# Cross-attention and two expert layers on one core: the first 256 tokens' down projection and batch 0's scores in native float32

## The chip, the cores and the metric

The kernel runs on one core of a Trainium2 chip. Its time is the device time of one execution, in microseconds (us). PE multiplies matrices, DVE and ACT do the elementwise work, POOL issues the indirect transfers, and SP issues all other transfers from one queue in program order.

## The reference

For each of 8 batches and 8 heads, 512 tokens and 32 state rows of 64 numbers read each other by softmax attention; the two results are joined to 4352 rows of 512. A first layer and a routed second one follow:

```python
scores = scale * np.matmul(x, state.transpose(0, 1, 3, 2))
...
xread = np.matmul(a, state)
...
sread = np.matmul(a2, x)
...
h = x @ w_in                      # 512 -> 2048
r = np.maximum(h, 0.0)
g = r * r
return (g @ w_out)                # 2048 -> 512
...
expert_idx = np.argmax(logits, axis=1)        # 8 experts
    h = np.maximum(x[mask] @ w1[e], 0.0)      # 512 -> 1024
    out[mask] = gate_w[mask, None] * (h @ w2[e])
```

w_in and w_out arrive as float64. The result has to be good to float32, since a token's expert is an argmax.

## The kernel before

Most products are done in float16 in three terms: each float32 operand is scaled by a power of two and split into a high and a low half (`split`, lines 306 to 312: ACT writes the high half, DVE the low one), and PE sums high x high, high x low and low x high in one bank.

The front. `weights` loads w_in and w_out as 16 blocks of 1 MB of float64 (`block`). `to_f32` turns each into float32 by bit operations (DVE lines 750, 752 and 763, ACT line 747). For w_in, `wi_scale` takes a block's own scale (ACT square, a sum on PE at line 787, DVE) and `wi_block` splits it. For w_out, `wo_square` sums the squares of every block; only when all eight are known do `weights` and `tensor_scale` make the one scale, and `wo_split` makes the halves (ACT line 863, DVE line 304). The float32 form of w_out's block q lies where the halves of block q + 2 will stand.

`attention(b)` makes batch b's scores. The product of state and w_in is formed first (`state_w`, line 550, tile sw), so that the up projection of a unit of 256 tokens is attention weights (aT) x sw: 8 steps c of 12 matmuls of 256 columns (lines 1174 to 1176), each step in one of two banks u. `hidden` evicts a step (ACT line 1137), squares it (ACT lines 1141 and 1143 for units 0 and 1) and takes the low half (DVE line 1148) into g_h and g_l. `down1` multiplies a tile of 128 tokens by w_out in 48 matmuls of 512 columns (lines 1226 to 1228); two tiles make a unit, and there are 17 units. `route_tile` squares a result (line 1013), splits it and turns it for the gate; records go to DRAM. `experts` prepares the second layer's weights beside this: loads, squares (line 941), splits, and writes of the halves.

The second layer (`moe2`) gathers 128 records at a time, multiplies them by an expert's halves and scatters the rows; at the steps in `DRAINED`, seven of them, POOL then drains.

The order on each engine is not written down but planned: each part is a generator that tells the class `Plan` which engine it needs and for how long, and `Plan.run` always lets the step go that could start first, then the one of lower priority number. Transfers are planned to land 2 us and their bytes over 350 GB/s after they are issued. The plan decides only the order; on the chip every engine takes its queue in that order and waits where it must.

Of the kernel before, what the change touches and what calls it, by code (L numbers as in the profile page):

```python
# [10 lines left out]
F32 = mybir.dt.float32  # L11
# [23 lines left out]
DRAINED = range(6, FULL + HALF - LAST - 2, 4)  # L35
# [22 lines left out]
TINY = 0.18  # L58

# [173 lines left out]
def moe_kernel(  # L233
# [108 lines left out]
    tiny1 = const.tile([128, 1], F32, name="tiny1")  # L342
    nc.gpsimd.memset(tiny1, float(2.0 ** -112))
# [6 lines left out]
    cg = const.tile([128, B + 1], F32, name="cg")  # L350
    icg = const.tile([128, B + 1], F32, name="icg")
    swi = const.tile([128, NB], F32, name="swi")
    iswi = const.tile([128, NB], F32, name="iswi")
    smin = const.tile([128, 2], F32, name="smin")
    ismin = const.tile([128, 2], F32, name="ismin")
# [14 lines left out]
    g_h = mw.tile([128, KF, 512], F16, name="g_h")  # L370
    g_l = mw.tile([128, KF, 512], F16, name="g_l")
# [57 lines left out]
    def attention(b):  # L429
# [32 lines left out]
        plan.add(group_bound(b, p), 3 if b else 1.2)  # L462
# [134 lines left out]
    def state_side(b, xh, xl, sth, stl, scl):  # L597
# [9 lines left out]
        for C in range(2):  # L607
# [119 lines left out]
    def to_f32(q, dst, squares):  # L727

        raw = raws.pop(q)
        if not W64:  # L730
# [7 lines left out]
            V.tensor_copy(dst, w)  # L738
            yield ev("wosq", q - NB)
# [147 lines left out]
    def experts():  # L887
# [23 lines left out]
        def fetch():  # L911
            for n in range(4 * NE):
# [14 lines left out]
                ev("stage", n).set(when)  # L927
# [23 lines left out]
        for i in range(2 * NE):  # L951
# [5 lines left out]
            for q in range(4):  # L957
# [13 lines left out]
                phl_slots.release(t)  # L971
# [36 lines left out]
    def route_tile(i, ps, k_h, rc, st):  # L1008

        j = i % 4  # L1010
        rc = rc.bitcast(F16)
        yield act(600)
        nc.scalar.activation(out=rc[:, 0:512].bitcast(BF16), in_=ps, func=AF.Square, accum_out=st["f2"][:, j:j + 1])
# [4 lines left out]
        pow2(s2, st["is2"][:, j:j + 1], f2, 204)  # L1018
        yield from split(rc[:, 0:512], rc[:, 512:1024], ps, s2, 600)
# [108 lines left out]
    def hidden(u, c, ps, k_h):  # L1128
# [3 lines left out]
        yield ev("cg", g)  # L1132
        yield r_slots
# [57 lines left out]
    def down1():  # L1191
        for u in range(NU):
            g = u // 2
            for j in range(2):
                i = 2 * u + j
                if i == 0:
                    yield ev("prepared")
                if i % 4 == 0:
                    m, recs, k_r = 4 if g < B else 2, [], []
                    st = {"f2": small.tile([128, 4], F32, name="f2"),  # L1200
                          "is2": small.tile([128, 4], F32, name="is2"),
                          "lg": small.tile([128, 4, NE], F32, name="lg")}
                at = plan.now()
                yield rec_slots
                plan.cur[2] = max(at, plan.now())
                k_r.append(rec_slots.last())
                recs.append(mg.tile([128, REC], F32, name=f"rec{k_r[-1] % RECS}", bufs=1))
                yield "pool", 0.1
                nc.gpsimd.tensor_copy(recs[-1][:, 513:514].bitcast(I32), rid[:, i:i + 1])
                plan.cur[2] = at  # L1210
                ts = slice((i % 4) * 128, (i % 4) * 128 + 128)
                at = plan.now()
                yield d_slots
                plan.cur[2] = max(at, plan.now())
                ps, k_h = ps_d.tile([128, 512], F32, name="d"), d_slots.last()
                for q in range(4):
# [3 lines left out]
                    if u == 0:  # L1220
# [467 lines left out]
```

## Time and profile before

| | us |
|---|---|
| three runs: median (lowest, highest) | 1135.59 (1133.19, 1138.03) |
| profiled execution: its own time | 1135.78 |
| its span, first to last instruction | 1133.9 |
| PE busy | 1030.1 (91%) |
| DVE busy | 706.8 (62%) |
| ACT busy | 583.7 (51%) |
| POOL busy | 130.4 (12%) |

A busy PE need not be at its best, since its matmuls overlap; the spacing of their starts tells more than their lengths. A line such as 304 or 326 is a helper's, so tiles tell which step it serves. L12 is line 12 of the kernel before.

### The profile page before, as it was taken

The numbers are of one execution on the slowest core, as the hardware profiler recorded it, in microseconds if no ns is written. First come the engines' busy times: TensorE is split into PE (matmuls) and PEld (weight loads), VectorE is DVE, ScalarE is ACT, GpSimd is POOL, SyncE is SP. The second block draws the span as 40 slices with busy tenths as digits, with TensorE's granted clock in tenths as the row PEclk, the third lists the DMA queues.
The fourth block names the chain that finished last, engine by engine and source line by source line (L and its number), as shares of the span: only waits on it lengthen the run. The fifth ranks groups of instructions, "written<-read, shape, count | busy, mean of one in ns | idle before, by whom it ended". The sixth has DMA issues, their size and how long they took to land. (4 is left out here: it accounts for less than half of the span.)

```text
span 1133.9 us, 26458 instructions
## 1 busy us (share of the span) xinstructions
PE 1030.1 (91%) x10707; PEld 664.6 (59%) x10707; DVE 706.8 (62%) x1838; ACT 583.7 (51%) x959; POOL 130.4 (12%) x149
## 2 busy tenths in 40 slices
PE   2255799999999999899999999999999999999998
PEld 1134355555556556465565566677777777677775
DVE  6989786978878878688787686546322222222222
ACT  6579777776777877677777776311101111010110
POOL 0200000110100100001002010122112112112111
PEclk9579699999999999999999999999999999999999
DMA  9335457477584696574755477773696776784692
GB/s 353 122 153 130 153 103 233 96 196 190 135 264 104 197 265 150 157 191 133 229 133 178 159 227 247 236 201 95 187 312 172 215 212 188 187 267 129 187 281 103
DMA packets 160544, 211.76 MB, mean 187 GB/s; under 512 B 112225, under 2 KB 113505, under 8 KB 155170
## 3 DMA queue, kind: packets, MB, share of 16 engines
q1 hardware_dynamic: 152098, 182.94, 57.2%
q0 software_dynamic: 8320, 27.08, 7.2%
q8 instruction: 86, 1.41, 0.5%
q14 instruction: 40, 0.33, 0.1%
HBM read 257.92 MB, written 51.68 MB: 273 GB/s over the span
## 5 line engine op out<-in xcount | busy, mean ns | idle before, releaser
L1496 ACT ACTIVATE r<-u 128x512 f32<-128x512 f32 x70 | 41.8, 597 | 326.1 <-PE u L1542 302.0
L1226 PE MATMUL d<-wo_t,g_h 128*128 128x512 f16 x544 | 208.0, 382 | 1.7 <-ACT wo_t L863 0.8
L1227 PE MATMUL d<-wo_t,g_h 128*128 128x512 f16 x544 | 208.1, 383 | 1.2 <-DVE wo_t L304 1.2
L1228 PE MATMUL d<-wo_t,g_l 128*128 128x512 f16 x544 | 208.2, 383 | 0.0
L1174 PE MATMUL u<-aT,sw 128*128 128x256 f16 x512 | 141.6, 277 | 26.3 <-ACT r L1137 23.4
L1176 PE MATMUL u<-aT,sw 128*128 128x256 f16 x512 | 141.6, 276 | 0.5 <-DVE sw L304 0.5
L1175 PE MATMUL u<-aT,sw 128*128 128x256 f16 x512 | 141.6, 277 | 0.0
L1137 ACT ACTIVATE r<-u,cg 128x512 f32<-128x512 f32 x136 | 92.6, 681 | 57.3 <-PE u L1176 34.1
L1499 DVE CAST hh<-r 128x512 f16<-128x512 f32 x70 | 30.2, 431 | 138.7 <-ACT r L1496 134.1
L1112 POOL DMA_INDIRECT rec_d<-rec,pi x34 | 38.7, 1138 | 564.3 <-DVE f L1016 176.6
L1148 DVE TENSOR_TENSOR g_l<-r,g_h 128x512 f16<-128x512 f32 x136 | 93.2, 686 | 7.0 <-ACT r L1143 5.6
L1510 DVE TENSOR_SCALAR o<-d,rec,wo_t 128x512 f32<-128x512 f32 x35 | 28.3, 810 | 107.4 <-PE d L1565 101.7
L1228 PEld LDWEIGHTS <-g_l 128*128 128x128 f16 x544 | 53.5, 98 | 66.9 <-issue 3.8
L1565 PEld LDWEIGHTS <-hh 128*128 128x128 f16 (+1 forms) x688 | 54.7, 102 | 56.9 <-issue 0.4
L1143 ACT ACTIVATE r<-r 128x512 f32<-128x512 f32 x136 | 85.3, 627 | 1.9
L1226 PEld LDWEIGHTS <-g_h 128*128 128x128 f16 x544 | 54.0, 99 | 53.6 <-issue 4.3
L1227 PEld LDWEIGHTS <-g_h 128*128 128x128 f16 x544 | 53.5, 98 | 53.3 <-issue 3.8
L1146 DVE CAST g_h<-r 128x512 f16<-128x512 f32 x120 | 50.8, 424 | 40.7 <-ACT r L1143 39.7
L1542 PE MATMUL u<-xes,stage 128*128 128x128 f16 x448 | 75.9, 219 | 0.0
L1541 PE MATMUL u<-xes,stage 128*128 128x128 f16 x448 | 75.9, 219 | 0.0
L1540 PE MATMUL u<-xes,stage 128*128 128x128 f16 x448 | 75.9, 219 | 0.0
L1175 PEld LDWEIGHTS <-sw 128*128 128x128 f16 x512 | 50.6, 99 | 39.2 <-issue 27.7
(334 smaller groups left out, 2685.8 us busy)
## 6 DMA issues: line engine op xcount, KB each, us to landing
w_d<-he SPq DMA_DIRECT2D x128, 256.0 KB
wo_t<-w_d SPq DMA_DIRECT2D x16, 2048.0 KB
stage<-w_d SPq DMA_DIRECT2D x14, 2048.0 KB
he<-w_d SPq DMA_DIRECT2D x14, 2048.0 KB
xx<-w_d SPq DMA_DIRECT2D x13, 2048.0 KB
sw<-w_d SPq DMA_DIRECT2D x13, 2048.0 KB
stage<-in_w_dram SPq DMA_DIRECT2D x20, 1024.0 KB
g_h<-w_d SPq DMA_DIRECT2D x8, 2048.0 KB
```

Of the source, the lines that this page charges most:

```text
L1137: nc.scalar.activation(out=r, in_=ps, func=AF.Relu, scale=cg[:, g:g + 1])
L1143: nc.scalar.activation(out=r, in_=r, func=AF.Square)
L1148: V.tensor_tensor(out=gl, in0=r, in1=gh, op=ALU.subtract)
L1174: mm(o, lhsT=hl[:, i, 0, fs], rhs=aT[:, i, :], start=i == 0, stop=False)
L1175: mm(o, lhsT=hl[:, i, 0, fs], rhs=aT[:, 2 + i, :], start=False, stop=False)
L1176: mm(o, lhsT=hl[:, i, 1, fs], rhs=aT[:, i, :], start=False, stop=i == 1)
L1226: mm(ps, lhsT=g_h[:, f, ts], rhs=w[:, 0, :], start=f == 0, stop=False)
L1227: mm(ps, lhsT=g_h[:, f, ts], rhs=w[:, 1, :], start=False, stop=False)
L1228: mm(ps, lhsT=g_l[:, f, ts], rhs=w[:, 0, :], start=False, stop=f == KF - 1)
L1540: mm(p[:, j, xs], lhsT=w[:, 0, k, fs], rhs=xe[:, k, xs], start=k == 0, stop=False)
L1541: mm(p[:, j, xs], lhsT=w[:, 0, k, fs], rhs=xe[:, 4 + k, xs], start=False, stop=False)
L1542: mm(p[:, j, xs], lhsT=w[:, 1, k, fs], rhs=xe[:, k, xs], start=False, stop=k == 3)
```

## The change

Unit 0 (256 tokens) no longer splits its hidden values or waits for w_out's halves: `hidden` writes one float32 square into the room of g_h and g_l (g32), and the new first part of `down1` multiplies it by the unsplit float32 blocks of w_out, as one native float32 matmul of 512 columns for each of 2 tiles and 16 rows of blocks: 32 instead of 96. For that `first_scales` makes w_in's least scale early and evens out the blocks' scales in the eviction (cgq), and `route_tile` applies w_out's scale to tiles 0 and 1 afterwards. `wo_split` now also waits until a block's float32 form has been used (down32). Batch 0's scores and its state side use x and the state in float32, without halves of x: 4 + 16 matmuls instead of 12 + 48; x and the state keep their room until then. The first block of w_in is loaded ahead of x. The plan takes the experts' loads and the writes of their halves to land 3 us later (LATE). Of the seven drains on POOL the one at step 30 is left.

```diff
--- before.py
+++ after.py
@@ -32,7 +32,7 @@
...
-DRAINED = range(6, FULL + HALF - LAST - 2, 4)
+DRAINED = (FULL + HALF - LAST - 5,)
@@ -56,6 +56,7 @@
...
+LATE = 3.0
@@ -367,8 +369,9 @@
...
-    g_h = mw.tile([128, KF, 512], F16, name="g_h")
-    g_l = mw.tile([128, KF, 512], F16, name="g_l")
+    g_t = mw.tile([128, 2, KF, 512], F16, name="g")
+    g_h, g_l = g_t[:, 0], g_t[:, 1]
+    g32 = g_t.bitcast(F32)
@@ -459,32 +462,40 @@
...
-        plan.add(group_bound(b, p), 3 if b else 1.2)
...
-        st_slots.release()
+        if b:
+            st_slots.release()
...
-        yield from splits([(xh[:, q], xl[:, q], xf[:, q], sxb[:, 0:1]) for q in (slice(0, 2), slice(2, 4))], 1024)
-        xf_slots.release()
-        plan.add(state_side(b, xh, xl, sth, stl, scl), PRIO_S0 if b == 0 else 1.7)
+        if b:
+            yield from splits([(xh[:, q], xl[:, q], xf[:, q], sxb[:, 0:1]) for q in (slice(0, 2), slice(2, 4))], 1024)
+            xf_slots.release()
+            pairs = ((sth, xh), (stl, xh), (sth, xl))
+        else:
+            pairs, scl = ((stt, xf),), eighth
+        plan.add(state_side(b, pairs, scl), PRIO_S0 if b == 0 else 1.7)
...
-        yield pe(48, 64)
+        yield pe(48, 64) if b else pe(64, 128)
...
-                a = xh[:, c, sb * 128:sb * 128 + 128]
-                mm(o, lhsT=a, rhs=sth[:, c, :], start=True, stop=False)
-                mm(o, lhsT=a, rhs=stl[:, c, :], start=False, stop=False)
-                mm(o, lhsT=xl[:, c, sb * 128:sb * 128 + 128], rhs=sth[:, c, :], start=False, stop=True)
+                ss_ = slice(sb * 128, sb * 128 + 128)
+                ops = [(x[:, c, ss_], a[:, c, :]) for a, x in pairs]
+                for n, (a, w) in enumerate(ops):
+                    mm(o, lhsT=a, rhs=w, start=n == 0, stop=n == len(ops) - 1)
+        if b == 0:
+            xf_slots.release()
+            st_slots.release()
@@ -827,9 +839,21 @@
...
-    def weights():
+    def first_scales():
 
         for q in range(NB):
+            yield ev("swi", q)
+        yield ev("cg", 0)
+        yield tiny(3)
+        V.tensor_reduce(out=smin[:, 0:1], in_=swi, axis=X, op=ALU.min)
+        V.tensor_reduce(out=ismin[:, 0:1], in_=iswi, axis=X, op=ALU.max)
+        V.tensor_scalar(out=cgq, in0=iswi, scalar1=smin[:, 0:1], scalar2=cg[:, 0:1], op0=ALU.mult, op1=ALU.mult)
+        ev("cgq").set()
+
+    def weights(q0=0):
+
+        plan.add(first_scales(), 0.5)
+        for q in range(q0, NB):
@@ -852,12 +874,12 @@
...
-        if W64:
-            yield ev("f32", q)
+        yield ev("f32", q)
...
             yield ev("wo", q - 2)
+            yield ev("down32", q - 2)
         w = wo[q + 2].rearrange("p a k d -> p (a k d)").bitcast(F32).rearrange("p (k d) -> p k d", k=2)
@@ -924,7 +946,7 @@
...
-                ev("stage", n).set(when)
+                ev("stage", n).set(when + LATE)
@@ -968,7 +990,7 @@
...
-                phl_slots.release(t)
+                phl_slots.release(t + LATE)
@@ -1009,13 +1031,18 @@
...
+        if i < 2:
+            yield ev("wo scale")
         yield act(600)
-        nc.scalar.activation(out=rc[:, 0:512].bitcast(BF16), in_=ps, func=AF.Square, accum_out=st["f2"][:, j:j + 1])
+        nc.scalar.activation(out=rc[:, 0:512].bitcast(BF16), in_=ps, func=AF.Square, accum_out=st["f2"][:, j:j + 1],
+                             scale=smin[:, 1:2] if i < 2 else 1.0)
         yield tiny(4)
...
+        if i < 2:
+            V.tensor_tensor(out=s2, in0=s2, in1=smin[:, 1:2], op=ALU.mult)
@@ -1130,13 +1157,22 @@
...
+        if u == 0:
+            yield ev("cgq")
...
-        nc.scalar.activation(out=r, in_=ps, func=AF.Relu, scale=cg[:, g:g + 1])
+        nc.scalar.activation(out=r, in_=ps, func=AF.Relu, scale=cg[:, g:g + 1] if u else cgq[:, c:c + 1])
         u_slots.release(k_h)
-        if u < 2:
+        if u == 0:
+            yield act(512)
+            nc.scalar.activation(out=g32[:, :, 2 * c:2 * c + 2, 0:128],
+                                 in_=r.rearrange("p f (a t) -> p a f t", a=2), func=AF.Square)
+            r_slots.release(k_r)
+            ev("g", u, c).set()
+            return
+        if u == 1:
@@ -1189,35 +1225,67 @@
...
-        for u in range(NU):
...
+        def end(i, ps, k_h, rec, st, m):
+            g = i // 4
...
+        yield ev("prepared")
+        first = []
+        for i in range(2):
+            first.append((yield from begin(i)))
+        for q in range(NB):
+            yield ev("f32", q)
+            yield ev("g", 0, q)
+            yield pe(16, 512)
+            w = wo[q + 2].rearrange("p a k d -> p (a k d)").bitcast(F32).rearrange("p (k d) -> p k d", k=2)
+            for i in range(2):
+                for f in range(2):
+                    mm(first[i][0], lhsT=g32[:, i, 2 * q + f, 0:128], rhs=w[:, f, :], start=q + f == 0,
+                       stop=q == NB - 1 and f == 1)
+            ev("down32", q).set()
+        for q in range(8):
+            ev("down", 0, q).set()
+        for i in range(2):
+            end(i, *first[i])
+        for u in range(1, NU):
...
+                ps, k_h, rec, s, m = yield from begin(i)
...
-                    if u == 0:
+                    if u == 1:
...
+                end(i, ps, k_h, rec, s, m)
@@ -1625,11 +1689,13 @@
...
     def start():
+        yield from block(0, wiv[:, :, 0:BW * WS], BW)
+        plan.add(wi_block(0), PRIO_WI)
         yield from load_x(0, 0)
         yield from load_st(0)
         yield from load(cs, cst, 1 << 17)
         yield from load(cs16, cst16, 1 << 16)
-        plan.add(weights(), 1)
+        plan.add(weights(1), 1)
```

The plan then puts the queues in another order. On PE, the first down block before follows the state matmuls of batch 1 (line 550's and 614's; t and S are banks, d a tile's result):

```order
L614 LDWEIGHTS sth
L614 MATMUL t<-xx,sth 64x512
L614 LDWEIGHTS sth
L614 MATMUL t<-xx,sth 64x512
L1226 LDWEIGHTS g_h
L1226 MATMUL d<-wo_t,g_h 128x512
L1227 LDWEIGHTS g_h
L1227 MATMUL d<-wo_t,g_h 128x512
L1228 LDWEIGHTS g_l
```

Now the first down block of float32 stands between up matmuls of unit 0 (line 1210 to 1212), ahead of the state matmuls for its last steps:

```order
L1211 MATMUL u<-aT,sw 128x256
L1212 LDWEIGHTS sw
L1212 MATMUL u<-aT,sw 128x256
L1272 MATMUL d<-wo_t,g 128x512 x4
L561 LDWEIGHTS sth
L561 MATMUL S<-wi_h,sth 32x512
L561 LDWEIGHTS sth
```

Eight such groups of 4 follow one another in this way, with the steps of units 0 and 1 between them; unit 1's first down block of float16 comes when unit 1's steps 0 to 6 are through.

On DVE, at the conversion of w_out's first blocks (wo_t; sw is the state's product, mt a maximum), before:

```order
L750 TENSOR_SCALAR wo_t<-wo_t 128x1024
L304 SCALAR_TENSOR_TENSOR sw<-S,sw 128x512
L621 TENSOR_REDUCE mt<-t 128x1
L752 SCALAR_TENSOR_TENSOR wo_t<-wo_t 128x1024
L304 SCALAR_TENSOR_TENSOR sw<-S,sw 128x512
L1148 TENSOR_TENSOR g_l<-r,g_h 128x2x256
L623 TENSOR_SCALAR mt<-mt,scl 128x1
L763 SCALAR_TENSOR_TENSOR wo_t<-wo_t 128x1024
L1148 TENSOR_TENSOR g_l<-r,g_h 128x2x256
L304 SCALAR_TENSOR_TENSOR sw<-S,sw 128x512
L750 TENSOR_SCALAR wo_t<-wo_t 128x1024
```

and now:

```order
L632 TENSOR_REDUCE mt<-t 128x1
L762 TENSOR_SCALAR wo_t<-wo_t 128x1024
L634 TENSOR_SCALAR mt<-mt,eighth 128x1
L764 SCALAR_TENSOR_TENSOR wo_t<-wo_t 128x1024
L305 SCALAR_TENSOR_TENSOR sw<-S,sw 128x512 x2
L632 TENSOR_REDUCE mt<-t 128x1
L775 SCALAR_TENSOR_TENSOR wo_t<-wo_t 128x1024
L634 TENSOR_SCALAR mt<-mt,eighth 128x1
L762 TENSOR_SCALAR wo_t<-wo_t 128x1024
L305 SCALAR_TENSOR_TENSOR sw<-S,sw 128x512 x2
```

Unit 0's low halves (g_l) are gone from between the conversions; unit 1's stand behind the last one.

On ACT, where the splits of w_out begin (swo is their scale, woacc the sums of squares), before:

```order
L1143 ACTIVATE r<-r 128x512
L443 ACTIVATE xx,ss<-stt 128x4x64
L821 ACTIVATE pjk,woacc<-stage 128x1024 x2
L309 ACTIVATE sth<-stt,sx 128x256
L318 ACTIVATE xx<-xx,sx 128x1024 x2
L555 ACTIVATE sw<-S 128x512
L863 ACTIVATE wo_t<-wo_t,swo 128x1024
L555 ACTIVATE sw<-S 128x512
L863 ACTIVATE wo_t<-wo_t,swo 128x1024 x5
```

and now:

```order
L885 ACTIVATE wo_t<-wo_t,swo 128x1024
L1170 ACTIVATE g<-r 128x2x2x128
L885 ACTIVATE wo_t<-wo_t,swo 128x1024
L444 ACTIVATE xx,ss<-xx 128x1024
L885 ACTIVATE wo_t<-wo_t,swo 128x1024
L446 ACTIVATE xx,ss<-stt 128x4x64
L885 ACTIVATE wo_t<-wo_t,swo 128x1024 x2
L1037 ACTIVATE rec_357,f_354<-d,ends 128x512
L1166 ACTIVATE r<-u,cg 128x512
L885 ACTIVATE wo_t<-wo_t,swo 128x1024
L1177 ACTIVATE g<-r 128x2x256
L1166 ACTIVATE r<-u,cg 128x512
```

The first splits stand ahead of the routing's square of tile 0 (line 1037, rec and f), and all of unit 1's evictions (line 1166 with cg) have come behind that square.

## Rows read from the trace of the kernel before

**Rows 1.** The page, part 2: busy tenths of PE and its granted clock in 40 slices.
```profile
PE   2255799999999999899999999999999999999998
...
PEclk9579699999999999999999999999999999999999
```
**Rows 2.** Stretches: from:to, length, busy us (instructions) of each engine, clock, DMA share, GB/s.
```profile
64.00:113.00 49.00, 31.30 (x312) 22.28 (x312) 43.09 (x65) 45.44 (x80) 0.00 (x0) 0.90 0.46 141
124.00:131.40 7.40, 6.14 (x28) 1.85 (x35) 6.86 (x10) 5.76 (x6) 0.00 (x0) 0.50 0.87 311
200.00:400.00 200.00, 193.82 (x1763) 115.30 (x1761) 166.00 (x453) 153.22 (x266) 19.74 (x24) 1.00 0.64 169
400.00:635.00 235.00, 223.78 (x1948) 132.59 (x1945) 183.21 (x501) 171.16 (x290) 18.05 (x24) 0.98 0.64 178
670.00:900.00 230.00, 230.00 (x2453) 162.65 (x2451) 107.20 (x353) 54.06 (x89) 44.93 (x45) 1.00 0.75 215
```
**Rows 3.** Timeline of PE, 124 to 141 us: start, length, instruction, count, [idle before <-releaser].
```profile
124.03 0.58 PE L1226 MATMUL d<-wo_t,g_h 128*128 128x512 f16 x1 [0.80 <-ACT wo_t L863]
125.85 0.59 PE L1227 MATMUL d<-wo_t,g_h 128*128 128x512 f16 x1 [1.23 <-DVE wo_t L304]
...
132.57 0.39 PE L1226 MATMUL d<-wo_t,g_h 128*128 128x512 f16 x1
...
140.14 0.38 PE L1228 MATMUL d<-wo_t,g_l 128*128 128x512 f16 x1
```
**Rows 4.** Timeline of DVE, 8 to 113 us.
```profile
9.88 0.69 DVE L750 TENSOR_SCALAR g_h<-g_h 128x1024 int32<-128x1024 int32 x1 [0.21 <-DMA g_h<-in_w_in_dram]
...
36.60 0.69 DVE L750 TENSOR_SCALAR xx<-xx 128x1024 int32<-128x1024 int32 x1
...
111.20 1.23 DVE L752 SCALAR_TENSOR_TENSOR stage<-stage 128x1024 int32<-128x1024 int32 x1
```
**Rows 5.** Timeline of ACT, 4 to 126 us.
```profile
6.05 1.06 ACT L441 ACTIVATE xx<-xx 128x1024 bf16<-128x1024 f32 x1 [0.18 <-DMA xx<-in_xT_dram]
...
117.51 1.11 ACT L821 ACTIVATE pjk<-stage 128x1024 bf16<-128x1024 f32 x1
...
122.83 1.15 ACT L863 ACTIVATE wo_t<-wo_t,swo 128x1024 f16<-128x1024 f32 x1 [0.35 <-DVE swo L847]
```
**Rows 6.** Timeline of PE, 144 to 146 us: float32 matmuls of 8 columns.
```profile
144.35 0.95 PE L988 MATMUL t<-emq,one 128*128 128x8 f32 x8
145.16 0.38 PE L1226 MATMUL d<-wo_t,g_h 128*128 128x512 f16 x1
```
**Rows 7.** Groups of weight loads by form: count | busy us, mean ns | idle before.
```profile
L1228 PEld LDWEIGHTS <-g_l 128*128 128x128 f16 x544 | 53.5, 98 | 66.9 <-issue 3.8
...
L988 PEld LDWEIGHTS t<-emq,one 128*128 128x128 f32 x8 | 1.1, 192 | 0.1
```
**Rows 8.** Groups of DVE, 8.5 to 113 us.
```profile
L1148 DVE TENSOR_TENSOR g_l<-r,g_h 128x512 f16<-128x512 f32 x15 | 10.3, 688 | 4.1 <-ACT r L1143 3.8
...
L304 DVE SCALAR_TENSOR_TENSOR xx<-xx,sx 128x1024 f16<-128x1024 f32 x4 | 5.0, 1278 | 0.0
```
**Rows 9.** Groups of ACT, 64 to 124 us.
```profile
L1137 ACT ACTIVATE r<-u,cg 128x512 f32<-128x512 f32 x16 | 10.8, 673 | 1.8 <-PE u L1176 1.7
L1143 ACT ACTIVATE r<-r 128x512 f32<-128x512 f32 x16 | 9.9, 622 | 0.0
```
**Rows 10.** Timelines of SP, ACT and PE, 447 to 459 us.
```profile
447.78 0.39 SPq L326 DMA_DIRECT2D wo_t<-in_w_dram  x1
...
456.54 1.06 ACT L941 ACTIVATE pjk<-wo_t 128x1024 bf16<-128x1024 f32 x1 [2.87 <-DMA wo_t<-in_w_dram]
...
458.31 0.27 PE L1174 MATMUL u<-aT,sw 128*128 128x256 f16 x1 [4.31 <-ACT r L1137]
```
**Rows 11.** Waits of PE, 135 to 640 us: us in total, times, longest.
```profile
PE u L1174 <- ACT r L1137: 15.7, 10, 4.3
```
**Rows 12.** Timeline of POOL, 826 to 842 us.
```profile
839.51 1.02 POOL L1466 DMA_INDIRECT rec<-rec_d,wo_t  x1 [10.61 <-issue]
```

More of the change, by code (lines that the diff above doesn't have):

```diff
@@ L353, in moe_kernel @@
     iswi = const.tile([128, NB], F32, name="iswi")
-    smin = const.tile([128, 2], F32, name="smin")
-    ismin = const.tile([128, 2], F32, name="ismin")
+    ends = const.tile([128, 4], F32, name="ends")
+    smin, ismin = ends[:, 0:2], ends[:, 2:4]
     swo = const.tile([128, NB], F32, name="swo")
@@ L461, in attention @@
         ev("sx", b).set()
-        plan.add(group_bound(b, p), 3 if b else 1.2)
+        plan.add(group_bound(b, p), 3 if b else 0.7)
         at = plan.now()
@@ L595, in group_scale, with state_side @@
         ev("cg", g).set()
-    def state_side(b, xh, xl, sth, stl, scl):
+    def state_side(b, pairs, scl):
         yield eb_slots
@@ L610, in state_side @@
             p = ps_t.tile([128, 512], F32, name="t")
-            yield "pe", 0.8
-            for a, x in ((sth, xh), (stl, xh), (sth, xl)):
+            yield "pe", 0.8 if b else 1.7
+            for n, (a, x) in enumerate(pairs):
                 for c in (2 * C, 2 * C + 1):
                     mm(p[64 * (c % 2):64 * (c % 2) + 64, :], lhsT=a[:, c, :], rhs=x[:, c, :],
-                       start=x is xh and a is sth, stop=x is xl)
+                       start=n == 0, stop=n == len(pairs) - 1)
             ps.append(p)
@@ L738, in to_f32 @@
             V.tensor_copy(dst, w)
+            ev("f32", q - NB).set()
             yield ev("wosq", q - NB)
@@ L1191, in down1, with begin @@
     def down1():
-        for u in range(NU):
-            g = u // 2
+        st = None
+        def begin(i):
+            nonlocal st
+            m = 4 if i // 4 < B else 2
+            if i % 4 == 0:
+                st = {"f2": small.tile([128, 4], F32, name="f2"),
+                      "is2": small.tile([128, 4], F32, name="is2"),
+                      "lg": small.tile([128, 4, NE], F32, name="lg"), "recs": [], "k_r": []}
+            at = plan.now()
+            yield rec_slots
+            plan.cur[2] = max(at, plan.now())
+            k_r = rec_slots.last()
+            st["k_r"].append(k_r)
+            rec = mg.tile([128, REC], F32, name=f"rec{k_r % RECS}", bufs=1)
+            st["recs"].append(rec)
+            yield "pool", 0.1
+            nc.gpsimd.tensor_copy(rec[:, 513:514].bitcast(I32), rid[:, i:i + 1])
+            plan.cur[2] = at
+            at = plan.now()
+            yield d_slots
+            plan.cur[2] = max(at, plan.now())
+            return ps_d.tile([128, 512], F32, name="d"), d_slots.last(), rec, st, m
@@ new lines, in end @@
+        def end(i, ps, k_h, rec, st, m):
+            g = i // 4
+            if i % 4 == 0:
+                plan.add(group_unscale(g), 1)
+            plan.add(route_tile(i, ps, k_h, rec, st), 2 if g < B else 0)
+            if i % 4 == m - 1:
+                plan.add(route_group(4 * g, m, st["recs"], st["k_r"], st), 2 if g < B else 0)
+        yield ev("prepared")
[12 more added lines that the diff above has]
+            ev("down32", q).set()
@@ L1203, in down1 @@
[L1203 to L1210, printed above, removed]
+                ps, k_h, rec, s, m = yield from begin(i)
                 ts = slice((i % 4) * 128, (i % 4) * 128 + 128)
-                at = plan.now()
@@ L1229, in down1 @@
                     ev("down", u, 4 * j + q).set()
-                if i % 4 == 0:
-                    plan.add(group_unscale(g), 1)
-                plan.add(route_tile(i, ps, k_h, recs[-1], st), 2 if g < B else 0)
-                if i % 4 == m - 1:
-                    plan.add(route_group(4 * g, m, recs, k_r, st), 2 if g < B else 0)
+                end(i, ps, k_h, rec, s, m)
         ev("moe1").set()
```

19 lines of the change are left out of this document (4 added, 15 removed).

## The prediction

> **What bounds the kernel now.** I read the page's forty slices first. PE is at 2 to 7 tenths in the first three slices and at 9 in nearly all that follow [rows 1]: a front of some 113 us, and behind it a stretch in which PE is never long idle. The table of stretches says the same in microseconds: 193.8 of 200 us and 223.8 of 235 in the long middle, 230.0 of 230 in the expert part, while DVE (166 of 200) and ACT (153 of 200) have slack [rows 2]. In the front it is the other way round: from 64 to 113 us PE works 31.3 of 49 us, DVE 43.1 and ACT 45.4 [rows 2]. So the time is (a) the moment from which PE can run through, (b) the matrix work left from there, and (c) the few holes behind.
>
> The moment is the first down matmul of unit 0, at 124.03 us [rows 3]. It waited for ACT's first split of w_out, which needs one scale over all of w_out, and so the last conversion on DVE. That is the chain: DVE converts float64 blocks from 9.88 us on, the last one's pattern is complete at 112.4 us (111.20 + 1.23) [rows 4], its squares begin at 117.51 us behind batch 1's squares on ACT, and the split runs at 122.83 us [rows 5].
>
> **The sum.** The profiled execution took 1135.8 us, of which 1133.9 are the span; the median of the three runs shown is 1135.6, so I make the sum against 1135.8.
>
> *1. Work that leaves the full stretch.* Unit 0's down projection (tiles 0 and 1) is 2 x 48 = 96 matmuls of 512 columns. From the one at 132.57 to the one at 140.14 us there are 35 steps, 0.216 us each [rows 3]: 96 x 0.216 = **-20.8 us**. In the new order PE reaches unit 1's first down block without 24 column-tiled state matmuls, 6 of the state side and the last 12 of the 256-column up matmuls, which the old order has behind it at that point; by the same spacing these are some 2.6 us, less 0.8 for the four small float32 matmuls that are now ahead (144.35 to 145.16 us [rows 6]): **+1.8**.
>
> *2. The float32 matmuls that replace them.* 32 of 512 columns. No row has such a one. The trace shows float32 only with 8 columns or fewer that matter: 4 instructions are 8 records, two each [rows 6], with weight loads of 192 ns against 98 for float16 [rows 7]. Bounds: two records at float16's pace, 2 x 0.216 = 0.43 us; or each record also reads its columns at half pace, as it does its weights (192/98), 0.86 us. I take 0.86, because the weight load is the nearest row and shows the half pace: 32 x 0.86 = 27.6 us, more than the 20.8 removed. It does not lie in the full stretch, though: 49 - 31.3 = 17.7 us of PE's front from 64 us on is idle [rows 2], and the time to 124 us is another 11. The Trainium skill, page FP8 and Floating Point Precision, section TensorE Precision Notes, says that true float32 takes 4 passes; no run here shows it. By it a matmul would be 4 x 0.216 = 0.86 us, and the sum would stay.
>
> *3. When unit 1's down block can start.* On DVE the change takes out of the way to the last conversion: unit 0's 8 subtractions for g_l, unit 1's (which the new order has behind the conversions), 15 in all up to 113 us at 0.69, and batch 0's two 128x1024 subtractions at 1.28 [rows 8]: 10.3 + 2.6 = 12.9, less about 0.08 of overlap each, so some 11.5 us. The first block of w_in ahead of x starts DVE earlier: 1 MB of x, issued first, was there at 6.05 us, w_in's block at 9.88 [rows 4, 5]; so 3.8 us, of which I count 1.5, as x now comes later and batch 0's first sums wait for it. The last conversion is then complete at 112.4 - 11.5 - 1.5 = 99.4 us, the two squares of 1.1 us at 102, and the scale, whose summing matmul stands in PE's own queue, at about 103.
>
> PE, in its new order, gets the w_out blocks one by one. Blocks 0 to 5 fit between their conversions (20.6 us of float32, 21 us of up matmuls in some 35 us of room from 68 us). Behind the scale's matmul stand 18 up matmuls (2 us), block 6 (3.4), 6 more (0.7) and block 7 (3.4): float32 ends at about 112.7 us. Now something new: ACT's queue has route_tile's first square, which needs all eight blocks, ahead of unit 1's evictions. From there to the eviction of unit 1's c=4, which frees the bank that c=6 needs, ACT has 5 evictions of 0.67, 8 squares of 0.62, 3 splits of 1.15 and 4 others of about 0.7 [rows 5, 9]; 14.6 us, less 0.1 of overlap each: 13 us. Then 12 up matmuls, 1.3 us. Unit 1's down starts at 112.7 + 13 + 1.3 = 127 us: **+3** against 124.
>
> *4. The slow clock there.* From 124 to 131.4 us the granted clock is 0.50, 1.2 GHz, after 11 us in which PE had worked little [rows 2]; so 7.4 us did 3.7 us of work, and two gaps of 0.80 and 1.23 us lie there too [rows 3]. In the new order PE has 13 us of up matmuls at ACT's pace in that place, about half busy, and at a like share (31.3 of 49) the clock was granted at 0.90 over 64 to 113 us. I take both back: **-5.7** (between 0 and -5.7).
>
> *5. Loads planned 3 us later.* One row shows what this is about: the expert load issued at 447.78 us is waited for by ACT until 456.54, and PE loses 4.31 us to it at 458.31 [rows 10], the longest of the 10 holes of 15.7 us in all from 135 to 640 us [rows 11]. The plan had put the square at about 5 us behind the issue; it took 8.8. Between 0 and -4.3: **-2**.
>
> *6. New holes.* Unit 2's up matmuls now come five blocks in a row (60 matmuls, 6.5 us) while ACT has 10 us of work between the same evictions, and PE has 20 us less in which DVE and ACT do the same work: DVE's 349 us of work in 435 us [rows 2] would then stand in 415, 84%. Between 0 and +8: **+4**.
>
> *7. One drain instead of seven.* POOL sat 10.61 us behind the drain at step 6 before its next gather [rows 12], yet PE is busy 230.0 of 230 us around it [rows 2]: **0**. The cover is the row of six record tiles; were it gone, the transposed records would be late and PE's up2 would wait. Batch 0's scores in float32 are 4 + 16 matmuls, which start at about 14 us behind the first block's and end at about 24 us (two column pairs of 1.7 us at the low clock, then 32 weight loads of 0.19 [rows 7]). DVE has 8 us of conversions queued ahead of the maximum that needs them, and SP's load of w_in block 5, which now waits for them, is first touched by DVE at 36.60 us today [rows 4]: **0**; without that cover up to 4 us.
>
> Sum: -20.8 + 1.8 + 3 - 5.7 - 2 + 4 = -19.7, so 1135.8 - 19.7 = **1116 us**.
>
> **The rivals.** *(a) The stretch is not PE's alone.* If ACT and DVE set the pace, what PE gains at 127 us comes back as holes before r's eviction, the releaser of 15.7 us of idle already [rows 11]. For it: both engines are in order and 73 to 83% busy. Against: PE idles only 17 of 435 us there [rows 2]. Given back by half to all: 1126 to 1136, about 1131.
>
> *(b) Slower: float32 at the low clock.* PE's queue now holds, between up matmuls, eight blocks that wait for DVE's conversions and ACT's squares, and behind each the state matmuls that DVE itself waits for. If PE idles there enough that 1.2 GHz is granted, as at 124 us, each float32 matmul is 1.73 us: 32 x 0.87 = 27.7 us more, of which 4 hide ahead of the scale's matmul: 1116 + 24 = 1140. It decides from a mean of 0.86 + (19.7 + 4)/32 = 1.6 us. Against: room of 35 us for 42 us of work keeps PE busy.
>
> *(c) Weight loads that do not overlap.* In the trace the float16 load of 98 ns hides in the spacing of 0.216 us [rows 3, 7]; if float32's two loads of 0.19 us do not, 32 x 0.38 = 12.2 us are added, 4 of them hidden: 1124. The Trainium skill says so for any load: page TensorE: Matmul & The Clock Gate, section The mechanism, that a weight load overlaps a matmul in flight only where the row group differs. The float16 rows do not agree with that.
>
> *(d) Better:* float32 at 0.43 us: blocks 6 and 7 end 3.4 us sooner, and if the loads give all 4.3 us and no new hole comes, 1116 - 3.4 - 2.3 - 4 = 1106.
>
> **How the numbers follow.** Forecast 0.60, (a) 0.16, (b) 0.10, (c) 0.08, (d) 0.06. A measurement can tell 0.5%, 5.7 us, from no change. Faster: all of (c) and (d), nearly all of the forecast and a third of (a), 0.78; the same: two thirds of (a) and edges of the rest, 0.12; slower: (b), 0.10. The likeliest time is 1116. The forecast's own bounds, terms 3 to 6 at their ends, are 1104 to 1126; the range takes in (c), (d)'s most and (a)'s most: 1102 to 1134.
>
> **What would show it.** Float32 down matmuls at 0.86 us spacing and a clock near 1.00 from 70 to 113 us; the last w_out square at about 102 us; unit 1's first down matmul at 123 to 130 us, with ACT's route square just ahead; no PE wait in the expert part. I am wrong if that matmul comes after 140 us, if PE's holes from 135 to 640 us grow past 25 us, or if the expert part waits for weights.

## The result, and the profile after

The changed kernel takes 1121.47 us in the median of four runs (1114.48 to 1124.46), the kernel before 1134.39 us (four runs, 1130.24 to 1138.03). The ratio is 0.9865, with a 95% interval of 0.9834 to 0.9897: 1.3% faster. The profiled execution is the fastest of the four: span 1112.6 us, 1114.48 us in all, 21.3 us below the one of before. It is set here beside a middling execution of before, so the parts below flatter the change: between the medians it is 12.9 us.

The stretches of before [rows 2], in the changed kernel (from:to, length, busy us of PE, PEld, DVE, ACT, POOL, then granted clock, DMA share, GB/s):

```profile
64.00:113.00 49.00, 47.85 (x306) 27.84 (x306) 41.32 (x67) 43.29 (x70) 0.00 (x0) 0.99 0.47 159
124.00:131.40 7.40, 7.40 (x58) 3.95 (x57) 6.60 (x19) 7.20 (x12) 0.00 (x0) 0.80 0.29 48
200.00:400.00 200.00, 193.61 (x1725) 114.55 (x1720) 160.22 (x417) 152.49 (x263) 14.89 (x21) 1.00 0.69 185
400.00:635.00 235.00, 231.24 (x2044) 140.01 (x2042) 194.62 (x544) 181.09 (x309) 18.00 (x24) 1.00 0.62 175
670.00:900.00 230.00, 223.98 (x2590) 162.06 (x2590) 98.80 (x324) 43.98 (x73) 42.80 (x42) 0.99 0.74 214
```

PE now works 47.85 of 49 us in the front, against 31.3, and the expert part, which had no idle time, has 6 us of it. PE's timeline of the changed kernel, 89 to 127 us and at the seam to the experts (start, length, instruction, count, idle before it and who released it):

```profile
89.19 3.60 PE L1272 MATMUL d<-wo_t,g 128*128 128x512 f32 x8
92.62 0.27 PE L1210 MATMUL u<-aT,sw 128*128 128x256 f16 x1
...
98.11 0.36 PE L901 MATMUL t<-fv,one 128*128 128x1 f32 x2
...
104.78 3.60 PE L1272 MATMUL d<-wo_t,g 128*128 128x512 f32 x8
108.22 0.28 PE L452 MATMUL t<-ss,one 128*128 128x3 f32 x2
...
123.71 0.37 PE L1210 MATMUL u<-aT,sw 128*128 128x256 f16 x1 [3.95 <-ACT r L1166]
...
126.22 0.63 PE L1294 MATMUL d<-wo_t,g 128*128 128x512 f16 x1
...
722.74 0.19 PE L1060 MATMUL t<-en_h,xr 128*128 128x8 f16 x1 [3.93 <-DMA xr<-rec]
```

Four float32 matmuls, eight records, take 92.62 - 89.19 = 3.43 us; the scale's matmul stands at 98.1 us, float32 ends at 108.2, and unit 1's first down matmul comes at 126.22 us. Ahead of it is a hole of 3.95 us, and behind the hole the last 12 up matmuls follow one another by 0.21 us in place of 0.11, 1.2 us more, at a granted clock of 0.52 from 124 to 127 us. The cause of the hole, in the timelines of ACT and DVE of the changed kernel:

```profile
109.23 0.67 ACT L1037 ACTIVATE rec<-d,ends 128x512 bf16<-128x512 f32 x1
...
122.97 1.29 ACT L1166 ACTIVATE r<-u,cg 128x512 f32<-128x512 f32 x2 [1.53 <-DVE g L1184]
```

```profile
118.39 0.16 DVE L1013 TENSOR_SCALAR env<-t 128x8 f32<-128x8 f32 x1
...
122.08 0.19 DVE L1023 TENSOR_TENSOR en_l<-emq,en_h 128x32 f16<-128x32 f32 x1
122.19 1.29 DVE L1184 TENSOR_TENSOR g<-r,g 128x512 f16<-128x512 f32 x2
```

The 19 small DVE instructions from 118.39 to 122.08 us prepare the expert embeddings; the subtractions that free r stand behind them.

### The profile page after: what moved, and what is told of

The parts are those of the page before. It is cut to its first block, busy times and chain, and to the rows that moved or that the text cites. A ratio compares the mean times of both kernels' runs of the same rounds, so it can differ in the third digit from the quotient of the medians.

```text
span 1112.6 us, 26342 instructions
## 1 busy us (share of the span) xinstructions
PE 1030.8 (93%) x10655; PEld 666.7 (60%) x10655; DVE 702.4 (63%) x1831; ACT 575.4 (52%) x949; POOL 128.7 (12%) x149
## 5 line engine op out<-in xcount | busy, mean ns | idle before, releaser
L1294 PE MATMUL d<-wo_t,g 128*128 128x512 f16 x512 | 194.3, 380 | 3.2 <-DVE rec L305 1.9
L1296 PE MATMUL d<-wo_t,g 128*128 128x512 f16 x512 | 194.1, 379 | 0.7 <-DVE g L1184 0.6
L1295 PE MATMUL d<-wo_t,g 128*128 128x512 f16 x512 | 194.2, 379 | 0.0
L1210 PE MATMUL u<-aT,sw 128*128 128x256 f16 x512 | 140.6, 275 | 16.6 <-ACT r L1166 13.8
L1166 ACT ACTIVATE r<-u,cg 128x512 f32<-128x512 f32 x128 | 87.2, 683 | 58.5 <-PE u L1212 36.5
L1574 DVE TENSOR_SCALAR o<-d,rec,wo_t 128x512 f32<-128x512 f32 x35 | 28.3, 810 | 106.6 <-PE d L1629 103.1
L1184 DVE TENSOR_TENSOR g<-r,g 128x512 f16<-128x512 f32 x128 | 87.6, 687 | 1.8 <-ACT r L1179 0.4
L1296 PEld LDWEIGHTS <-g 128*128 128x128 f16 x512 | 50.1, 98 | 62.2 <-DVE g L1184 2.3
L1294 PEld LDWEIGHTS <-g 128*128 128x128 f16 x512 | 50.3, 98 | 50.7 <-DVE g L1182 2.3
L1179 ACT ACTIVATE r<-r 128x512 f32<-128x512 f32 x128 | 79.9, 627 | 1.5
L1295 PEld LDWEIGHTS <-g 128*128 128x128 f16 x512 | 50.1, 98 | 49.3 <-issue 2.3
L1604 PE MATMUL u<-xes,stage 128*128 128x128 f16 x448 | 78.0, 222 | 0.7 <-issue 0.7
L1605 PE MATMUL u<-xes,stage 128*128 128x128 f16 x448 | 78.0, 222 | 0.0
L1606 PE MATMUL u<-xes,stage 128*128 128x128 f16 x448 | 78.0, 222 | 0.0
L1604 PE MATMUL u<-xes,xx 128*128 128x128 f16 x416 | 70.6, 219 | 0.5 <-DMA xes<-rec 0.5
L1606 PE MATMUL u<-xes,xx 128*128 128x128 f16 x416 | 70.5, 219 | 0.0
```

The costliest lines, as they stand in the source:

```text
L1179: nc.scalar.activation(out=r, in_=r, func=AF.Square)
L1184: V.tensor_tensor(out=gl, in0=r, in1=gh, op=ALU.subtract)
L1210: mm(o, lhsT=hl[:, i, 0, fs], rhs=aT[:, i, :], start=i == 0, stop=False)
L1294: mm(ps, lhsT=g_h[:, f, ts], rhs=w[:, 0, :], start=f == 0, stop=False)
L1295: mm(ps, lhsT=g_h[:, f, ts], rhs=w[:, 1, :], start=False, stop=False)
L1296: mm(ps, lhsT=g_l[:, f, ts], rhs=w[:, 0, :], start=False, stop=f == KF - 1)
```

## The experiments

Each kernel was timed in five rounds beside the kernel before, in three groups of runs. The kernel before had a median of 1138.1 us in the first (from the mark to x first), 1134.7 in the second (scores in float16, only the down projection, half of the float32 work, 96 matmuls less with the old orders) and 1137.0 in the third (the others), so between groups the ratios compare and not the medians; 0.01 is some 11.4 us. The mark is the changed kernel once more: 1122.3 us, ratio 0.9859 (0.9827 to 0.9891).

> The changed kernel once more, as the mark for the three that follow and for the spread between executions. Forecast: 1114 to 1125 us, as its four runs so far. In its profile the matmul stretch from unit 1's first down block on has 20 to 25 us of PE idle time, and the wait for the transposed record of the last-but-one tile (3.9 us at 722.74 us in the profile so far) comes back if it is a matter of the order, and not if it was a chance of one execution.

Its profile spans 1119.9 us, 7.3 more than the first of the same kernel, with the same orders. 3.0 us of that lie in the front, of which the last section tells. The wait at the seam came back with 2.8 us: it belongs to the order. Below, starts are compared with the profile of the changed kernel that has the same front.

**LATE 0:**

```diff
-LATE = 3.0
+LATE = 0.0
```

> LATE is 0 in place of 3: expert loads are again planned to land 3 us earlier. My theory (term 5): +2 us, between 0 and +4.3, with a PE hole of 2 to 4 us behind an ACT square that waits for its load. Rival: the table only reshuffles small holes, and the time is within 2 us either way, with no wait of ACT for a stage load over 2 us. The wait for xr at 722 us is in this stretch too: if the later loads caused it, it is gone here.

1128.23 us, 0.9930 (0.9905 to 0.9954): 5.9 us above the mark by the medians, 8 by the ratios. ACT's waits for loads, 135 to 640 us (us in total, times, longest), of the kernel before, of the changed one and with LATE 0:

```profile
ACT pjk L941 <- DMA stage<-in_w_dram: 7.0, 5, 2.2
ACT pjk L941 <- DMA wo_t<-in_w_dram: 4.6, 4, 2.9
```

```profile
ACT pjk L963 <- DMA stage<-in_w_dram: 1.3, 1, 1.3
ACT pjk L963 <- DMA wo_t<-in_w_dram: 0.2, 1, 0.2
```

```profile
ACT pjk L963 <- DMA stage<-in_w_dram: 7.3, 5, 3.6
```

The mechanism of term 5 is there: before, ACT waits 11.6 us for expert loads, with the 3 us 1.5 (2.9 in the second profile), without them 7.3. The whole is larger than the term's bound, but not all of it is this mechanism. PE's holes between the first and the last down matmul of the layer are 23.9 us against 14.7 and 17.2, and one of them is a wait of 4.6 us for a gathered record (xes) at the seam, where the wait for xr is gone. The expert weights end at 670.0 us, 21 us earlier than in the changed kernel.

**Seven drains:**

```diff
-DRAINED = (FULL + HALF - LAST - 5,)
+DRAINED = range(6, FULL + HALF - LAST - 2, 4)
```

> All seven drains of GpSimd are back. My theory (term 7): 0, within 2 us, since PE stays busy around each of them behind six record tiles. Rival: each costs a wait of PE for transposed records, 6 x 1 us or more, at or over +6 us, and PE's idle time behind 740 us grows by as much.

1122.68 us, 0.9877 (0.9848 to 0.9905): the same as the mark, as expected.

**x first,** in start():

```diff
-        yield from block(0, wiv[:, :, 0:BW * WS], BW)
-        plan.add(wi_block(0), PRIO_WI)
         yield from load_x(0, 0)
...
-        plan.add(weights(1), 1)
+        plan.add(weights(), 1)
```

> x is loaded ahead of w_in's first block again; nothing else is changed. My theory (term 3): DVE's first conversion 3.8 us later, the last one 1.5 us later, and unit 1's first down matmul with it: +1.5 us. Rival A: PE is busy from 64 to 108 us anyway and the start is set by ACT's and DVE's queues behind the route square, so 0. Rival B: all 3.8 us come through.

1123.06 us, 0.9879 (0.9851 to 0.9907). The time can't tell 1.5 us from 0; the profile can: the scale's matmul comes at 103.1 us against 101.1 and unit 1's first down matmul at 130.1 against 129.2. My theory holds for the conversions, and rival A for half of what follows.

**Scores in float16.** The hunks of attention() and state_side() are taken back:

```diff
-            pairs, scl = ((stt, xf),), eighth
+        pairs = ((sth, xh), (stl, xh), (sth, xl))
...
-        yield pe(48, 64) if b else pe(64, 128)
+        yield pe(48, 64)
```

> Batch 0's scores go back to float16 pairs; the rest of the change stays. My theory: DVE has the two subtractions of 1.28 us in front of the conversions again and ACT two splits, the last conversion is 2.6 us later, PE has the shorter matmuls, so +2.6 us (0 to +4). Rival: the float32 scores hold DVE and w_in's block 5 back by as much as they save, so 0 or below.

1140.19 us, 1.0048 (1.0031 to 1.0064): by the ratios some 21 us above the mark, slower than the kernel before. Neither theory has that. Its profile, the longest of its runs (1145.81 us), against the mark's: the scale comes 3.7 us later, unit 1's first down matmul at 134.5 us, 5.3 later, the layer from there takes 4.2 us more, and 14.4 are lost behind its last down matmul. The stores of prepared expert weights, SP's row of w_d (duration min/median/max, first and last start), in the kernel before, in the changed one and in this run:

```profile
L326 SPq DMA_DIRECT2D w_d<-he x128: 332/382/1343, 162.0 to 702.6; - x128
```

```profile
L327 SPq DMA_DIRECT2D w_d<-he x128: 332/386/1546, 156.8 to 691.2; - x128
```

```profile
L327 SPq DMA_DIRECT2D w_d<-he x128: 332/376/1305, 153.8 to 728.4; - x128
```

PE's waits in this run, 713 to 770 us:

```profile
PE u L1597 <- DMA stage<-w_d: 10.3, 1, 10.3
PE t L1053 <- DMA xr<-rec: 4.6, 1, 4.6
```

The planner's new order ends the preparation of the expert weights 31 to 37 us later, and PE stands 10.3 us for the first weights.

**Only the float32 down projection.** The four edits above together.

> Only the float32 down projection is left of the change: scores, order of loads, LATE and the drains are as before. My theory: it is what carries the gain, -20.8 + 1.8 - 5.7 + 4 and a start some 6 us later than in the prediction's sum without the other parts, so 6 us above the changed kernel, some 1127 us (ratio to the kernel before 0.993). Rival A: the other parts carry nothing, and it equals the changed kernel (0.9865). Rival B: without them the front is too late for the float32 work, and the ratio is 1.0 or above.

1132.74 us, 0.9987 (0.9972 to 1.0001): no gain by itself. The 20.8 us leave the stretch, but the scale comes at 110.4 us, float32 ends at 114.6 and unit 1's first down matmul comes at 137.3 us, 13.3 later than the first one of before. From there to the layer's last it takes 603.3 us in place of 621.0, and the experts' part 4.5 us more: 13.3 - 17.7 + 4.5, nothing.

**Only the float32 scores.** The kernel before with the hunks of attention() and state_side().

> The kernel before with batch 0's scores in float32 and nothing else of the change. Theory 1 (the two float32 parts need each other: the scores shorten the front by some 5 us, as unit 1's first down matmul at 134.5 us without them against 129.2 with them shows, and the float32 down projection uses the front): 3 to 6 us faster, ratio 0.995 to 0.997, unit 0's first down matmul at 118 to 121 us in place of 124.0. Theory 2: the scores carry the whole gain, ratio 0.984 to 0.988. Theory 3: the loss without them (scores16) was the order of the expert part alone, and here nothing is gained, 0.999 to 1.002.

1133.49 us, 0.9975 (0.9957 to 0.9993). Unit 0's first down matmul is at 125.4 us, not earlier than 124.03, and the layer's last at 741.1 against 745.03. Theory 2 falls. Between the sizes of theory 1 (up to 0.997) and theory 3 (from 0.999) the interval doesn't decide, and the way of theory 1, an earlier start, isn't there. The two parts alone are worth 1.5 and 2.8 us by their ratios; the whole change is worth 15 to 16.

**Half of the float32 work.** The inner loop over f goes, so that only f = 0 is multiplied:

```diff
-                for f in range(2):
-                    mm(first[i][0], lhsT=g32[:, i, 2 * q + f, 0:128], rhs=w[:, f, :], start=q + f == 0,
-                       stop=q == NB - 1 and f == 1)
+                mm(first[i][0], lhsT=g32[:, i, 2 * q, 0:128], rhs=w[:, 0, :], start=q == 0, stop=q == NB - 1)
```

> Leaves out 16 of the 32 float32 down matmuls (every second one: half of the hidden columns of the first 256 tokens). 13.7 us of PE work less. My theory: the matmuls ahead of the scale over w_out are hidden behind the conversions, only blocks 6 and 7 count, 4 x 0.86: the time falls by 3.4 us (0 to -4), and unit 1's first down matmul comes at 122 to 126 us. Rival: float32 is on the path, and the time falls by 10 to 13.7 us.

1119.17 us, 0.9863 (0.9838 to 0.9887): 13.7 us of PE work less give 3.1 us by the medians and nothing by the ratios. Unit 1's first down matmul comes at 127.7 us against 129.2 (122 to 126 was expected, from the profile whose start is 3 us earlier). The float32 work is hidden, as term 2 has it.

**96 matmuls less in the middle**, first with all orders as they are, then with the planner told (`yield pe(8 if u in SKIP else 12, 512)`):

```diff
+SKIP = (5, 6, 7)
...
-                        mm(ps, lhsT=g_l[:, f, ts], rhs=w[:, 0, :], start=False, stop=f == KF - 1)
+                        if u not in SKIP:
+                            mm(ps, lhsT=g_l[:, f, ts], rhs=w[:, 0, :], start=False, stop=f == KF - 1)
```

> Leaves out the third product (low half of the hidden values with the high half of w_out) of units 5, 6 and 7: 96 matmuls of 512 columns fewer in the middle of the matmul stretch, the same number that the change takes out. My theory: the stretch is PE's, so 96 x 0.216 = 20.8 us less. Rival (a) of the prediction: ACT and DVE set the pace there, half or all comes back as holes before r's eviction, and the time falls by 0 to 10 us.

> The same 96 products of units 5, 6 and 7 are left out as in skip96, and the planner is told: it counts 8 matmuls per step there in place of 12 and writes the orders of all engines anew. If the 16 us that came back in skip96 were due to an order written for other lengths: 12 to 20 us below the changed kernel, 1102 to 1110 us. If ACT, DVE and the transposes set the pace there as soon as PE has less: again 3 to 8 us below it, 1114 to 1119 us.

The first takes 1115.86 us, 0.9828 (0.9802 to 0.9854): 3 to 6 us less of 20.8. Rival (a) is right about the middle. PE's timeline, 320 to 400 us, shows what the time became:

```profile
324.12 0.38 PE L902 MATMUL t<-fv,one 128*128 128x1 f32 x2 [1.94 <-ACT he L638]
...
374.55 0.19 PE L1061 MATMUL t<-en_h,xr 128*128 128x8 f16 x1 [4.29 <-DMA xr<-rec]
...
395.29 0.18 PE L1061 MATMUL t<-en_h,xr 128*128 128x8 f16 x1 [1.22 <-DMA xr<-rec]
```

From the first to the last down matmul it needs 590.0 us against 594.2. The work there is 19.1 us less, but PE is idle 12.3 us more, and 2.5 us more are lost to a granted clock of 0.50, in part right at the end of the wait of 4.29 us.

The second takes 1136.04 us, 0.9996 (0.9980 to 1.0012), slower than with the 96 matmuls. From the first to the last down matmul it needs 587.0 us against 591.5, so a new order wins 4.5 of the 20.8, as little as the old one (work -20.6, idle +10.3, slow clock +5.7); then PE, done at 713.0 us, waits for weights whose last store is at 718.3. PE's waits there, 713 to 770 us:

```profile
PE u L1606 <- DMA stage<-w_d: 16.6, 1, 16.6
PE t L1061 <- DMA xr<-rec: 5.1, 1, 5.1
PE t L1118 <- DVE oh L1109: 4.7, 1, 4.7
```

**LATE 6:**

```diff
-LATE = 3.0
+LATE = 6.0
```

> LATE is 6 in place of 3. Going from 3 to 0 cost some 7 us. If a square or store behind a load that lands late is what the 3 us remove, and the longest landing was 8.8 us against some 5 planned, 6 us remove what is left: 1 to 4 us below the changed kernel. Rival: 3 us cover it and the rest is the luck of one order: within 3 us either way. Second rival: the weights of the expert part come later, and PE waits for a stage load behind 720 us: 3 us or more above.

1144.70 us, 1.0076 (1.0058 to 1.0094): the second rival, many times its size. The layer itself is as fast (592.1 us from the first to the last down matmul, holes 12.8), but the last store comes at 733.6 us. PE's waits, 713 to 770 us:

```profile
PE t L1060 <- DMA xr<-rec: 9.6, 1, 9.6
PE u L1604 <- DMA stage<-w_d: 8.7, 1, 8.7
PE t L1117 <- DVE oh L1108: 5.8, 1, 5.8
```

**Embeddings later,** in embeddings():

```diff
-        yield ev("wo scale")
+        yield ev("g", 1, 7)
```

> The expert embeddings' 19 small DVE instructions (118.4 to 122.2 us in the changed kernel's profile) are planned behind unit 1's last low half. My theory: the subtraction that frees r comes 3.8 us earlier, the PE hole of 3.95 us ahead of unit 1's last up matmuls is gone, and the time falls by 2 to 4 us. Rival: the first tiles' logits come later, one transposed record holds its one buffer longer, and PE waits for xr instead: 0 or above.

1148.02 us, 1.0125 (1.0099 to 1.0152). The hole of 3.95 us is gone and unit 1's first down matmul comes at 123.1 us, 3.1 earlier: the cause of that hole is shown. All of it and far more is lost behind: 12.0 us between the down matmuls, 7.2 of them to a granted clock of 0.50, and 23.4 at the seam and after it. SP's timeline and PE's waits at the seam:

```profile
727.92 0.37 SPq L1510 DMA_DIRECT2D stage<-w_d  x1
...
735.75 12.66 SPq L1051 DMA_TRANSPOSE xr<-rec  x1
```

```profile
PE t L1060 <- DMA xr<-rec: 27.5, 2, 26.8
```

The last store is at 724.8 us, four loads of weights follow it on SP's queue, and the transpose of the record behind them.

The seam in all runs (us):

| kernel | last store of weights | layer's last down matmul | experts' first matmul | median | ratio |
|---|---|---|---|---|---|
| before | 702.6 | 745.0 | 745.2 | 1134.4 | 1 |
| changed | 691.2 | 717.8 | 718.0 | 1121.5 | 0.9865 |
| changed again | 696.9 | 723.5 | 724.3 | 1122.3 | 0.9859 |
| LATE 0 | 670.0 | 736.2 | 719.6 | 1128.2 | 0.9930 |
| seven drains | 698.2 | 724.8 | 725.3 | 1122.7 | 0.9877 |
| x first | 698.8 | 725.3 | 729.1 | 1123.1 | 0.9879 |
| scores in float16 | 728.4 | 732.9 | 743.5 | 1140.2 | 1.0048 |
| only down projection | 697.8 | 740.6 | 740.8 | 1132.7 | 0.9987 |
| only scores | 694.8 | 741.1 | 741.4 | 1133.5 | 0.9975 |
| half of the float32 work | 694.6 | 721.2 | 725.0 | 1119.2 | 0.9863 |
| 96 less | 692.8 | 719.4 | 719.6 | 1115.9 | 0.9828 |
| 96 less, planned | 718.3 | 713.0 | 731.5 | 1136.0 | 0.9996 |
| LATE 6 | 733.6 | 718.3 | 744.9 | 1144.7 | 1.0076 |
| embeddings later | 724.8 | 726.6 | 755.9 | 1148.0 | 1.0125 |

The four runs with a last store behind 715 us are the four in which PE stands for over 12 us from 713 to 770 us (15 to 28 us, in the others at most 6). An early end alone does not make a kernel fast: LATE 0 has the earliest.

## Why the prediction was right, and where not

The time lies in the range, 5.5 us above the 1116 us. Its parts, in us, from the two profiles of the changed kernel against the one of before. Work is PE's busy time, less half of it where the granted clock is 0.50; that half is the slow clock's part. The parts are rounded.

| | forecast | first profile | second |
|---|---|---|---|
| start (term 3) | +3 | +2.2 | +5.2 |
| work from there on (terms 1 and 2) | -19.0 | -16.5 | -16.5 |
| slow clock and gap at the start (term 4) | -5.7 | -4.0 | -3.9 |
| slow clock later | no term | -2.5 | -1.8 |
| idle time later (terms 5 and 6) | +2 | -0.4 | +3.0 |
| sum | -19.7 | -21.3 | -14.0 |

The row without a term is what I overlooked. In the kernel before the granted clock fell three more times in the layer, to 0.50, 1.2 GHz, each time at the end of a PE hole or within 1.3 us of it: holes of 4.31 us [rows 10], 2.32 and 2.49 us. Stretches of the kernel before, its second and third hole, and a stretch of the changed kernel behind its hole at the seam:

```profile
459.20:462.60 3.40, 3.40 (x10) 1.20 (x9) 3.03 (x9) 2.19 (x5) 0.37 (x2) 0.50 0.40 121
534.30:537.69 3.39, 3.39 (x34) 1.45 (x33) 2.50 (x5) 3.38 (x6) 2.36 (x3) 0.50 0.96 271
609.40:612.78 3.38, 3.08 (x22) 1.79 (x22) 2.41 (x5) 3.20 (x6) 1.99 (x4) 0.50 0.25 89
```

```profile
533.01 0.27 PE L1174 MATMUL u<-aT,sw 128*128 128x256 f16 x1 [2.32 <-ACT r L1137]
...
609.70 0.37 PE L1174 MATMUL u<-aT,sw 128*128 128x256 f16 x1 [2.49 <-ACT r L1137]
```

```profile
720.83:727.64 6.81, 4.90 (x56) 4.90 (x57) 0.87 (x2) 1.04 (x2) 0.00 (x0) 0.50 1.01 367
```

PE worked 9.9 us in the three, at half pace: 5.0 us lost. In the changed kernel's layer nothing of this kind is left behind the start; in its expert part 2.5 us are lost in the last stretch.

- **Terms 1 and 2 hold in their mechanism**, 2.5 us too large. From the first float16 down matmul to the layer's last it takes 591.5 us in place of 621.0, 29.5 less: 16.9 of work, 7.7 of slow clock, 4.8 of idle time. So the other work that the new order has behind the start was not 1.8 us but some 3.9. A float32 matmul takes 3.43/4 = 0.857 us, forecast 0.86, at a clock of 0.99. The Trainium skill's 4 passes (page FP8 and Floating Point Precision, section TensorE Precision Notes) agree: 4 x 0.216 = 0.86. Rival (b) needed 1.6 us.
- **Rival (c) falls.** 64 float32 weight loads of 190 ns, 12.2 us, add nothing to 8 x 3.43 us. The Trainium skill's line that a load overlaps only where the row group differs (page TensorE: Matmul & The Clock Gate, section The mechanism) does not hold for these rows either; the same section also lets a load into the background weight buffer overlap.
- **Term 3 holds in its size, by luck**: 126.2 us in one profile and 129.2 in the other, forecast 127, out of two errors that cancel. Float32 ended 4.5 us sooner than I had it (the last square of w_out starts at 95.5 us, not at 102), and from its end to unit 1's down matmul it took 18.0 us in place of 14.3, with the hole of 3.95 behind the embeddings on DVE and 1.2 at the slow clock. The 21 us of up matmuls that I put ahead of the scale are all 192; 102 of them came behind it.
- **Term 4 holds in its way and was too large.** The gap of 0.80 us lies ahead of 124.03, where term 3 starts to count, and the 7.4 us at half pace hold the gap of 1.23 already: from 124.03 on there were some 4.4 us to take back, and all but 0.3 to 0.5 came.
- **Term 5 was too small.** Forecast -2, at most -4.3; undoing it costs 5.9 us, of which part is at the seam. I priced it by PE's one long hole [rows 10]; ACT's nine waits for loads, 11.6 us, were the rows to read, and beside them the slow clock behind that hole.
- **Term 6 was wrong in place.** No new holes in the layer: 14.0 us from 135 to 640 us (16.6 in the second profile), against 17.7. They came in the expert part (8.0 us for 4.9), where I said there would be no PE wait: 3.9 us for a transposed record. Idle time and slow clock behind the start together gave -2.9 and +1.2 in the two profiles, forecast +2.
- **Term 7** holds for the drains. For the scores it failed: at most 4 us if the cover went, and 2.6 in term 3, against some 21 us in the run that takes them back.

The forecast's own bounds, 1104 to 1126, are not terms 3 to 6 at their ends: by its figures these are some 1106 and 1131. The range holds both.

The step that failed is that each edit has a price of its own. The sum was near for the whole, in part by luck: work and term 4 were put 4.2 us too large, and slow clock that it did not see made up for 2. Taken apart, the down projection is worth 1.5 us: its work leaves the layer there too (21.0 us less), but its 27.4 us of float32 end where the front does, and alone the scale comes at 110.4 us against 98.1 and 101.1. Loading x first and taking the scores in float16 cost 2.0 and 3.7 us of that, each tried by itself; the rest was not taken apart. And the sum had no line for the seam. The first weight load is issued 2.3 to 4.9 us behind the last store, and where PE waited for the weights the first expert matmul came 11 to 15 us behind that store. By that estimate the weights could have been there before at 714 to 718 us, 27 to 31 us ahead of PE; in the changed kernel, at 702 to 706 us, some 12 to 15 ahead. An edit that delays them by more shows in the time.

Rival (a) got 0.16 and is half right: in the middle of the layer 14 to 17 of 20.8 us of PE work come back, 10 to 12 of them as waits on ACT, DVE and transposed records and the rest mostly as slow clock, with either order. The work that the change removes did not come back. That this is because it stood at the start, where unit 0's evictions were long done, is my reading and was not tried by itself.

The median lies above the profile by 7 us, and the second profile says where: 3.0 us in the front, 2.7 more between the down matmuls, 1.5 at the seam and behind.

Still open is which rows of the planner's order decide whether the weights end at 691 or at 730 us; a version with the embeddings later and the preparation held early was not tried. No version that was run beats the changed kernel with the whole computation.

## What to carry to other kernels

Work moved into an idle front is free only if what ends the front comes sooner too: alone, 27.4 us of float32 in place of 20.8 us of float16 gave nothing. A hole in the bounding engine can cost more than its length: here three holes of 2.3 to 4.3 us went with 10 us at half pace, 5.0 us more, so count the clock beside the idle time. When the bounding engine gets faster, look at the next place where it meets another chain, and write down that chain's end and its slack. Where a planner writes the order, one constant redraws all queues: edits of 3 or 4 us moved the end of the weights by up to 42 us and the time by up to 26, so that end has to be read from a trace for each such edit. It does not say everything: with LATE 0 it came 21 us sooner and the kernel was 6 us slower.

## What the runs showed of the hardware

The 16 float32 matmuls of batch 0's scores (32 records) took 3.79 us in one profile of the changed kernel and 7.09 in the other, with the same order and the same instructions ahead. PE's timeline, 14 to 27 us, of the first and then of the second:

```profile
18.27 3.79 PE L495 MATMUL S<-stt,xx 128*128 128x64 f32 x32
21.89 0.60 PE L799 MATMUL u<-pjk,oneb 128*128 128x256 bf16 x4
```

```profile
18.81 7.09 PE L495 MATMUL S<-stt,xx 128*128 128x64 f32 x32
25.69 1.06 PE L799 MATMUL u<-pjk,oneb 128*128 128x256 bf16 x4
```

By the starts the 32 records take 3.62 us and 6.88 us, a factor of 1.9, near that between 2.4 and 1.2 GHz. Yet the granted clock reads 0.70 from 20 to 40 us in the first and 1.00 in the second. In the second that is not a reading: the trace's first record of the clock begins there at 68.7 us (at 17.7 in the first), and time without a record counts as 1.00. So in the front the durations, not that column, tell the level. It costs 3 us, as DVE waits for these scores; its timeline in the second profile, where the first has no wait:

```profile
25.93 1.22 DVE L507 TENSOR_REDUCE mx<-S 128x32 f32<-128x1024 f32 x1 [1.99 <-PE S L495]
```

What decides which of the two comes is open.
